# Two thin tiles of a mixture-of-experts stage: pinned on every engine, transposed through the score tiles, one weight tile in another buffer

## The chip, the core and the metric

The kernel runs on one core of a Trainium2 chip. The metric is the device time of one execution in microseconds (us). Before the change three executions took 421.13, 422.70 and 427.82 us; the median is 422.7 us. The execution that the profile was taken of is a further one: 420.79 us, of which the span from its first to its last instruction is 419.0 us.

## The reference

The inputs are q, k and v (4 batches, 8 heads, 768 positions, 64 wide), a decay per head, and the weights of a mixture of 8 experts. The first part is a decaying linear attention, worked in blocks. Its output is a matrix of 3072 tokens by 512. The second part sends each token to one expert:

```python
logits = x @ w_gate + modality_bias[modality_id]
e_idx = np.argmax(logits, axis=1)
...
for e in range(E):
    mask = e_idx == e
    h = np.maximum(x[mask] @ w1[e], 0.0)
    out[mask] = gate_w[mask, None] * (h @ w2[e])
```

w1 of one expert is 512 by 1024, w2 is 1024 by 512: 2 MB each in fp32.

## The kernel before, in words

**Stages.** The attention runs first, and the tokens are written to DRAM (`xs`) with their gate logits. On the way each token gets a slot in a table `inv`, sorted by expert. The second part goes over tiles of tokens of one expert. A wide tile has 256 tokens; a thin one has 64 (`XT`) or 32 (`FEW`). The order is: wide tile 0, wide tile 1, the two thin tiles, and then ten or more wide tiles. The change touches what stands between the layers of wide tile 1 and the first wide tile behind the thin ones: `run_early`.

**A wide tile** gathers its rows (POOL, indirect DMA into `xg`), transposes them on PE (L614) into the PSUM tiles `x` and `kv`, and splits them into a high and a low part (`xh` on ACT, `xl` on DVE). Its weights arrive in `raw1` and `raw2` and are split into `w1h`, `w1l` and `w2h`, `w2l` in four quarters each (ACT L553 the high part, DVE L554 the low part). Each product is then three matmuls (L627, L630, L631). The first layer writes the PSUM tiles `s`, the second layer `o`.

**A thin tile** uses plain fp32 and no split. `turn_few` transposes its rows (`xq` to `xf`). `thin_first` multiplies them by w1 (L662), several column strips side by side, and ACT applies the ReLU into `hn` (L666). `thin_turn` transposes `hn` on PE (L673), and DVE copies the result to `hnt` (L675). `thin_second` multiplies by w2 (L687), ACT scales it (L691) and POOL scatters it to the output (L695).

**Where weights of the thin tiles lie.** The 64-token tile takes its weights from `raw1` and `raw2`, where they arrive under a condition: if the tile has the same expert as the one before it, the transfer is skipped and the old contents serve. The 32-token tile's weights are always loaded. Before the change `fetch_both` puts its w1 in the buffer of `w1h` and its w2 in the buffer of `w1l`, which are free as soon as the first layer of wide tile 1 is over.

**Order.** Each engine executes its queue in order. `pinned` ties an instruction behind the last pinned one of its engine; what isn't pinned is placed by the scheduler of the framework. Weights are fetched by SP, whose queue is in order too: an instruction that waits there holds up all behind it. The first of the fetches in question waits until the gather of the next tile's rows has landed (`fetch_w1(..., gathered)`).

Of the kernel before, what the change touches and what calls it, by code (L numbers as in the profile page):

```python
# [6 lines left out]
F32 = mybir.dt.float32  # L7
F32R = mybir.dt.float32r
BF16 = mybir.dt.bfloat16
I32 = mybir.dt.int32  # L10
AF = mybir.ActivationFunctionType
# [4 lines left out]
P = 128  # L16
# [4 lines left out]
LOADS = 3  # L21
# [19 lines left out]
def linear_attention_moe(tc, qkv, lam, modality, wg, mbias, w1, w2, out):  # L41
    nc = tc.nc
    with ExitStack() as ctx:
# [10 lines left out]
        def behind(later, first, wait=True):  # L54

            info = (mybir.DependencyInfo(mybir.DependencyClass.Sync, mybir.DependencyReason.DATA) if wait else
                    mybir.DependencyInfo(mybir.DependencyClass.NoSync, mybir.DependencyReason.SCHED_ONLY))
            tc.add_manual_dep(later.ins, first.ins.name, info, reason="order")
# [493 lines left out]
        def split(src, hi, lo, pin=False):  # L552
            cp = nc.scalar.copy(out=hi, in_=src)  # L553
            df = nc.vector.tensor_tensor(out=lo, in0=src, in1=hi.bitcast(F32), op=ALU.subtract)  # L554
            if pin:
                pinned(cp)
                pinned(df)
            return cp, df
# [28 lines left out]
        def fetch_regs(lst, i, always):  # L587
            er = nc.sync.value_load(item(lst, 0, i), min_val=0, max_val=E - 1)
            if always:
                return er, {}  # L590
            cr = nc.sync.value_load(item(lst, 2, i), min_val=0, max_val=1)
            return er, {"cond": cr}
# [10 lines left out]
        def fetch_w1(er, kw, after=None, to=None):  # L603
            fetch_halves(raw1_all if to is None else to, w1, er, kw, after)

        def fetch_w2(er, kw, after=None, to=None):
            fetch_halves(raw2_all if to is None else to, w2, er, kw, after)
# [14 lines left out]
        def turn_rows(cols, before=None, part=range(2), pin=False):  # L622
            for i in part:
                split(*turn_part(i, cols, before, pin))
# [28 lines left out]
        def thin_first(x, w):  # L653

            m = x.shape[-1]
            ways = P // m
            hp = ps.tile([P, 8, P], F32, name="s", bufs=2)[:, : FC // ways]
            per = max(1, 4 // ways)
            for q in range(per):
                for kc in range(KC):  # L660
                    for fh in range(ways):
                        mm = nc.tensor.matmul(hp[fh * m : (fh + 1) * m, 2 * q : 2 * q + 2, :].rearrange("p a f -> p (a f)"),  # L662
                                              x[:, kc, :], w[per * fh + q][:, kc, :], start=(kc == 0), stop=(kc == KC - 1),
                                              tile_position=(0, fh * m))
            hn = work.tile([P, FC // ways, P], F32, name=f"hn{m}", bufs=1)
            nc.scalar.activation(out=hn, in_=hp, func=AF.Relu)  # L666
            return hn, mm

        def thin_turn(hn, mm):
            n = hn.shape[1]  # L670
            tp = ps.tile([P, n, P], F32, name=("x", "kv")[n // 4], bufs=1)
            for f in range(n):
                behind(nc.tensor.transpose(out=tp[:, f, :], in_=hn[:, f, :], identity=ident), mm, wait=False)  # L673
            hnt = work.tile([P, n, P], F32, name=f"hnt{n}", bufs=1)
            nc.vector.tensor_copy(out=hnt, in_=tp)  # L675
            return hnt

        def thin_second(idx, hnt, w2, m):

            ways = P // m  # L680
            w = DM // ways
            yp = ps.tile([P, w], F32, name="o", bufs=2)
            for f in range(FC):
                a, b = divmod(f, 2)
                fh, f4 = divmod(f, hnt.shape[1])
                for j in range(ways):
                    mm = nc.tensor.matmul(yp[j * m : (j + 1) * m], hnt[:, f4, fh * m : (fh + 1) * m],  # L687
                                          w2[a][:, b, j * w : (j + 1) * w], start=(f == 0), stop=(f == FC - 1),
                                          tile_position=(0, j * m))
            y = work.tile([P, w], F32, name=f"yn{m}", bufs=1)  # L690
            nc.scalar.activation(out=y, in_=yp, func=AF.Copy, scale=idx[:, 0, 1:2].bitcast(F32))  # L691
            to = work.tile([P, 1], I32, name="to", bufs=THIN)
            nc.vector.tensor_scalar(out=to, in0=idx[:, 0, 0:1], scalar1=float(ways), scalar2=strip[:, m // XT :][:, :1],
                                    op0=ALU.mult, op1=ALU.add)
            sc = nc.gpsimd.indirect_dma_start(  # L695
                out=out.rearrange("t (n w) -> (t n) w", n=ways),
                out_offset=bass.IndirectOffsetOnAxis(ap=to, axis=0),
                in_=y, in_offset=None, bounds_check=ways * N - 1, oob_is_err=False)
            apart("tokens", sc)
            return mm  # L700

        def second(idx, whole):
            for t in range(2):
# [32 lines left out]
        def turn_few(x, rows):  # L736
            m = x.shape[-1]
            tp = ps.tile([P, KC, m], F32, name=("x", "kv")[m // XT], bufs=1)
            for kc in range(KC):
                nc.tensor.transpose(out=tp[:, kc, :], in_=rows[:, kc * (P + E) : kc * (P + E) + P], identity=ident[:m, :m])  # L740
            return nc.vector.tensor_copy(out=x, in_=tp)

        def fetch_both(er, kw):

            first, second = parts(F32)
            second = second.rearrange("p i k f -> p i (k f)").rearrange("p i (f n) -> p i f n", f=2)
            fetch_w1(er, kw, to=first)
            fetch_w2(er, kw, to=second)
            return quarters(first), quarters(second)

        def quarters(t):
            return [t[:, i] for i in range(4)]
# [5 lines left out]
        def parts(dt):  # L758

            return [work.tile([P, 4, KC, TT], dt, name=nm, bufs=1) for nm in ("w1h", "w1l")]  # L760
# [187 lines left out]
        def regs(n):  # L948
            return fetch_regs(*tiles[n][1:], False)
# [8 lines left out]
        fixed_ones = EARLY + THIN + MIN_WIDE  # L958
        wides = EARLY + THIN
        idxs = {}  # L960
        before = None

        def rows_of(n):

# [5 lines left out]

        def run(n):
            idx = idxs.get(n) or get_idx(n)
            turned = wide(first_tail if n == 0 else tail, before, True)
            if n + 1 < fixed_ones:
                ahead = range(EARLY, wides + 1) if n == 0 else range(n + 2, min(n + 3, fixed_ones))
                if n == 0:
                    turn_rows(TT, turned, pin=True)
                    for i in range(4):
                        split(raw1[i], w1h[i], w1l[i], True)
                    late_list(*begun[2], exA, nA)  # L980
                    fetch_w2(*regs(n + 1))
                for m in ahead:
                    idxs[m] = get_idx(m)
                if n > 0:
                    fetch_w2(*regs(n + 1))
                    turn_rows(TT, turned, pin=True)
                for m in ahead:
                    gathered = rows_of(m)
                if n > 0:
                    for i in range(4):  # L990
                        split(raw1[i], w1h[i], w1l[i], True)
                if n + 2 < fixed_ones:
                    fetch_w1(*regs(n + 2), gathered)
            second(idx, turned)

        def run_early(n):

            nonlocal w1h, w1l, before
            idx = idxA[n]
            whole = wide(tail, pin=True)  # L1000
            fetch_w2(*regs(EARLY))
            both = fetch_both(*fetch_regs(*tiles[EARLY + 1][1:], True))
            turn_few(xf[0], xq[0])
            second(idx, whole)
            turn_few(xf[1], xq[1])
            hn, _ = thin_first(xf[0], raw1)
            fetch_w1(*regs(wides))
            other, mm = thin_first(xf[1], both[0])
            hnt = [thin_turn(hn, mm)]
            turn_rows(TT, part=(0,))  # L1010
            mm = thin_second(idxs[EARLY], hnt[0], raw2, XT)
            hnt.append(thin_turn(other, mm))
            turn_rows(TT, mm, part=(1,))
            gathered = rows_of(wides + 1)
            fetch_w2(*regs(wides))
            before = thin_second(idxs[EARLY + 1], hnt[1], both[1], FEW)
            w1h, w1l = (quarters(t) for t in parts(F32R))
            for i in range(4):
                split(raw1[i], w1h[i], w1l[i])
            fetch_w1(*regs(wides + 1), gathered)  # L1020

        for n in range(fixed_ones):
# [67 lines left out]
```

## Time and profile before

| | |
|---|---|
| median of three executions | 422.7 us (421.13 to 427.82) |
| profiled execution | 420.79 us, span 419.0 us |
| PE busy | 396.8 us (95% of the span) |
| DVE busy | 252.6 us (60%) |
| ACT busy | 181.3 us (43%) |
| POOL busy | 114.4 us (27%) |
| mean granted clock of TensorE | 0.985 |

PE is the matmul engine TensorE, PEld its weight loads, DVE VectorE, ACT ScalarE, POOL GpSimd, SP the engine that issues most transfers. A name such as L687 is a line of the kernel before. In rows of an engine's order, `o<-raw,hnt` means that the instruction writes `o` and reads `raw` and `hnt`; the profile's names leave out numbers, so `raw` is `raw1` or `raw2`. A bracket at a row's end tells how long the engine had been idle, and on whom it waited. A granted clock of 1.00 is TensorE's upper level, 2.4 GHz, and 0.50 its lower, 1.2 GHz.

### The profile page before, as it was taken

Reading aid. Unit: us, or ns where it says so; the run is one execution under the profiler, and the core shown is the slowest. Engines: PE = TensorE matmul, PEld = TensorE weight load, DVE = VectorE, ACT = ScalarE, POOL = GpSimd, SP = SyncE. Lnnn points to the kernel's source line nnn. Section 1 sums busy time; section 2 is a strip of 40 time slices with the busy share of each in tenths; the row PEclk is TensorE's granted clock in tenths of the full one; section 3 lists DMA queues with packets and bytes.
Section 4 is the critical chain, followed back from the end, with each engine's and each line's share of the span. In section 5 each row is a group of like instructions: output and inputs, shape, how many; then the busy total and the mean of one; then the engine's idle time right before and its main releaser. Section 6 shows DMA issues by size and latency. Waiting matters only on the chain.

```text
span 419.0 us, 9681 instructions
## 1 busy us (share of the span) xinstructions
PE 396.8 (95%) x3864; PEld 354.4 (85%) x3864; DVE 252.6 (60%) x435; ACT 181.3 (43%) x273; POOL 114.4 (27%) x117
## 2 busy tenths in 40 slices
PE   8799999999899999899999999999999999999970
PEld 4599999889798986698989899898989898998950
DVE  5678687879689731476473828374664838273600
ACT  1123323325446432455463827364555638273410
POOL 5010144263178530322040222213040402202010
PEclk9999999999899999999999999999999999999995
DMA  6999999995910129122026775302020111101010
GB/s 208 329 387 388 391 358 349 332 386 196 337 54 4 60 66 395 59 53 80 25 71 235 240 265 159 146 14 70 25 80 25 55 50 46 50 3 52 2 34 12
DMA packets 23348, 63.82 MB, mean 152 GB/s; under 512 B 6901, under 2 KB 8445, under 8 KB 21248
## 3 DMA queue, kind: packets, MB, share of 16 engines
q1 hardware_dynamic: 15056, 43.36, 28.8%
q0 software_dynamic: 4768, 13.08, 9.8%
q10 hardware_dynamic: 3472, 6.69, 4.1%
q8 instruction: 32, 0.52, 0.5%
q14 instruction: 20, 0.16, 0.1%
HBM read 91.40 MB, written 14.07 MB: 252 GB/s over the span
## 4 chain that ended last, share of the span: by engine, by line
issue 44%; POOL 9%; DMA 8%; SPq 2%; DVE 0%; POOLq 0%
POOL out_dram L711 6%; DMA idx<-inv 4%; DMA xg<-xs,idx 4%; POOL xg L579 3%; SPq L567 1%; SPq L597 1%; POOL out_dram L695 0%; SPq L564 0%; POOLq L579 0%; POOLq L711 0%; DVE ats L538 0%; DVE listB L540 0%; DVE atB L438 0%; SPq L569 0%; DVE listB L541 0%
## 5 line engine op out<-in xcount | busy, mean ns | idle before, releaser
L631 PE MATMUL s<-xh,w1l 128*128 128x256 f32 x384 | 107.8, 281 | 1.0 <-DVE w1l L554 1.0
L627 PE MATMUL s<-xh,w1h 128*128 128x256 f32 x384 | 108.1, 281 | 0.0
L630 PE MATMUL s<-xl,w1h 128*128 128x256 f32 x384 | 107.6, 280 | 0.0
L645 DVE SCALAR_TENSOR_TENSOR hl<-s,hh 128x512 fp32r<-128x512 f32 x48 | 33.2, 691 | 81.0 <-ACT hh L644 81.0
L627 PE MATMUL o<-w2h,hh 128*128 128x512 f32 x192 | 75.8, 395 | 0.0
L631 PE MATMUL o<-w2h,hl 128*128 128x512 f32 x192 | 74.8, 390 | 0.0
L630 PE MATMUL o<-w2l,hh 128*128 128x512 f32 x192 | 74.8, 389 | 0.0
L631 PEld LDWEIGHTS s<-xh,w1l 128*128 128x128 f32 x384 | 73.5, 191 | 1.2 <-DVE w1l L554 1.2
L627 PEld LDWEIGHTS s<-xh,w1h 128*128 128x128 f32 x384 | 72.2, 188 | 1.8 <-ACT hh L644 0.8
L630 PEld LDWEIGHTS s<-xl,w1h 128*128 128x128 f32 x384 | 72.1, 188 | 0.4
L554 DVE TENSOR_TENSOR w2l<-raw,w2h 128x1024 fp32r<-128x1024 f32 x48 | 58.8, 1224 | 10.6 <-ACT w2h L553 10.6
L644 ACT ACTIVATE hh<-s 128x512 fp32r<-128x512 f32 x48 | 28.8, 599 | 71.0 <-PE s L631 68.4
L711 POOL DMA_INDIRECT out_dram<-y,idx x20 | 28.1, 1403 | 98.2 <-ACT y L710 93.8
L554 DVE TENSOR_TENSOR w1l<-raw,w1h 128x1024 fp32r<-128x1024 f32 x46 | 53.4, 1219 | 0.9 <-PE o L687 0.8
L553 ACT CAST w2h<-raw 128x1024 fp32r<-128x1024 f32 x48 | 49.9, 1039 | 0.0
L579 POOL DMA_INDIRECT xg<-xs,idx x20 | 24.4, 1218 | 84.6 <-PE kv L614 79.7
L553 ACT CAST w1h<-raw 128x1024 fp32r<-128x1024 f32 x46 | 45.1, 1065 | 0.0
L631 PEld LDWEIGHTS o<-w2h,hl 128*128 128x128 f32 x192 | 36.0, 188 | 7.6
L630 PEld LDWEIGHTS o<-w2l,hh 128*128 128x128 f32 x192 | 36.1, 188 | 7.2
L627 PEld LDWEIGHTS o<-w2h,hh 128*128 128x128 f32 x192 | 36.1, 188 | 7.2
L389 POOL DMA_INDIRECT inv<-pay,sloti x24 | 32.8, 1365 | 23.0 <-PE x L296 5.6
L710 ACT ACTIVATE y<-o,idx 128x512 f32<-128x512 f32 x20 | 13.8, 690 | 52.4 <-PE o L631 42.5
(216 smaller groups left out, 472.1 us busy)
## 6 DMA issues: line engine op xcount, KB each, us to landing
raw<-in_w_dram SPq DMA_DIRECT2D x52, 1024.0 KB
load<-in_qkv_dram SPq DMA_DIRECT2D x11, 2048.0 KB
xs<-xn ACTq DMA_DIRECT2D x24, 272.0 KB
load<-in_qkv_dram SPq DMA_DIRECT2D x4, 512.0 KB
w1h<-in_w_dram SPq DMA_DIRECT2D x2, 1024.0 KB
w1l<-in_w_dram SPq DMA_DIRECT2D x2, 1024.0 KB
dk<-tab_d SPq DMA_DIRECT2D x2, 256.0 KB
inv<-pad SPq DMA_DIRECT2D x2, 196.0 KB
```

The costliest lines, as they stand in the source:

```text
L389: sc = nc.gpsimd.indirect_dma_start(out=inv, out_offset=bass.IndirectOffsetOnAxis(ap=at, axis=0), in_=pay[:, c, :], in_offset=None)
L553: cp = nc.scalar.copy(out=hi, in_=src)
L554: df = nc.vector.tensor_tensor(out=lo, in0=src, in1=hi.bitcast(F32), op=ALU.subtract)
L567: nc.sync.dma_start(out=idx[p : p + cols, 0, :], in_=inv[bass.ds(vr, cols), 0:2])
L579: last = nc.gpsimd.indirect_dma_start(out=(to or xg)[t][:m], out_offset=None, in_=xs[:rows, :], in_offset=bass.IndirectOffsetOnAxis(ap=idx ...
L627: mm = pinned(nc.tensor.matmul(out, ah, bh, start=first, stop=False))
L630: pinned(nc.tensor.matmul(out, ah, bl, start=False, stop=False))
L631: return pinned(nc.tensor.matmul(out, al, bh, start=False, stop=last))
L644: act = nc.scalar.activation(out=hh[i], in_=hp, func=AF.Relu)
L645: low = nc.vector.scalar_tensor_tensor(out=hl[i], in0=hp, scalar=0.0, in1=hh[i].bitcast(F32), op0=ALU.max, op1=ALU.subtract)
L710: nc.scalar.activation(out=y, in_=yp, func=AF.Copy, scale=idx[:, t, 1:2].bitcast(F32))
L711: sc = nc.gpsimd.indirect_dma_start(out=out, out_offset=bass.IndirectOffsetOnAxis(ap=idx[:, t, 0:1], axis=0), in_=y, in_offset=None, bound ...
```

## The change

All instructions of the thin tiles on PE, ACT and DVE are pinned in the order of the code. The transposes of `hn` go to PSUM tiles of the kind `s` instead of `x` and `kv`. The code of `run_early` is in another order: both first layers, then the transposes of both thin tiles with those of the next wide tile's rows, then its splits, then both second layers. The 32-token tile's w2 goes to a third buffer of the pool `load` (`w2f`), which no one else uses by then; its w1 stays in the buffer of `w1h`. Its w2 is now fetched ahead of the 64-token tile's w2, and its w1 behind it.

```diff
+            pinned(nc.scalar.activation(out=hn, in_=hp, func=AF.Relu))
...
-            tp = ps.tile([P, n, P], F32, name=("x", "kv")[n // 4], bufs=1)
+            tp = ps.tile([P, 8, P], F32, name="s", bufs=2)[:, :n]
...
             whole = wide(tail, pin=True)
+            few = fetch_regs(*tiles[EARLY + 1][1:], True)
+            w2f = work.tile([P, 4, 2, DM], F32, name="w2f", tag="load", bufs=LOADS)
+            fetch_w2(*few, to=w2f)
             fetch_w2(*regs(EARLY))
-            both = fetch_both(*fetch_regs(*tiles[EARLY + 1][1:], True))
+            w1f = work.tile([P, 4, KC, TT], F32, name="w1h", bufs=1)
+            fetch_w1(*few, to=w1f)
+            both = quarters(w1f), quarters(w2f)
             turn_few(xf[0], xq[0])
             second(idx, whole)
             turn_few(xf[1], xq[1])
-            hn, _ = thin_first(xf[0], raw1)
+            hns = [thin_first(xf[0], raw1)]
             fetch_w1(*regs(wides))
-            other, mm = thin_first(xf[1], both[0])
-            hnt = [thin_turn(hn, mm)]
-            turn_rows(TT, part=(0,))
-            mm = thin_second(idxs[EARLY], hnt[0], raw2, XT)
-            hnt.append(thin_turn(other, mm))
-            turn_rows(TT, mm, part=(1,))
+            hns.append(thin_first(xf[1], both[0]))
+            hnt = [thin_turn(hns[0])]
+            parts0 = turn_part(0, TT, pin=True)
+            hnt.append(thin_turn(hns[1]))
+            parts1 = turn_part(1, TT, pin=True)
+            split(*parts0)
+            split(*parts1)
+            w1h, w1l = (quarters(t) for t in parts(F32R))
+            split(raw1[0], w1h[0], w1l[0], True)
+            split(raw1[1], w1h[1], w1l[1], True)
+            thin_second(idxs[EARLY], hnt[0], raw2, XT)
             gathered = rows_of(wides + 1)
             fetch_w2(*regs(wides))
-            before = thin_second(idxs[EARLY + 1], hnt[1], both[1], FEW)
-            w1h, w1l = (quarters(t) for t in parts(F32R))
-            for i in range(4):
-                split(raw1[i], w1h[i], w1l[i])
+            split(raw1[2], w1h[2], w1l[2], True)
+            thin_second(idxs[EARLY + 1], hnt[1], both[1], FEW)
+            split(raw1[3], w1h[3], w1l[3], True)
             fetch_w1(*regs(wides + 1), gathered)
```

**PE between the layers of wide tile 1 and the next wide tile.** `hn64` and `hnt4` belong to the 64-token tile, `hn32` and `hnt2` to the 32-token tile; `w1h` in an L662 row holds the small tile's w1. Before:

```order
L662 MATMUL s_2459<-raw1_122,xf0_138 64x256 x16
L614 MATMUL x_2524<-ident_91,xg0_126 128x128
...
L662 MATMUL s_2498<-w1h_2381,xf1_139 32x256 x16
L673 MATMUL kv_2517<-ident_91,hn64_2476 128x128 x4
L687 MATMUL o_2531<-raw2_123,hnt4_2522 64x256 x16
L673 MATMUL x_2555<-ident_91,hn32_2515 128x128 x2
L614 MATMUL kv_2560<-ident_91,xg0_126 128x128
...
L687 MATMUL o_2604<-w1l_2382,hnt2_2558 32x128 x32
```

and now:

```order
L662 MATMUL s_2459<-raw1_122,xf0_138 64x256 x16
L1027 TENSOR_LOAD nums_151
L662 MATMUL s_2498<-w1h_2384,xf1_139 32x256 x16
L673 MATMUL s_2517<-ident_91,hn64_2476 128x128 x4
L614 MATMUL x_2524<-ident_91,xg0_126 128x128
...
L673 MATMUL s_2529<-ident_91,hn32_2515 128x128 x2
L614 MATMUL kv_2534<-ident_91,xg0_126 128x128
...
L687 MATMUL o_2549<-raw2_123,hnt4_2522 64x256 x16
L687 MATMUL o_2612<-w2f_2361,hnt2_2532 32x128 x32
```

The small tile's first layer comes directly behind the other's, all transposes stand together, and both second layers stand last.

**SP, the fetches for the thin tiles**, of which each row left out is a second half of the same transfer or a register instruction. Before:

```order
L597 DMA raw1_122<-in_w1_dram 128x2048
...
L597 DMA raw2_123<-in_w2_dram 128x2048
...
L597 DMA w1h_2381<-in_w1_dram 128x2048
...
L597 DMA w1l_2382<-in_w2_dram 128x2048
...
L569 DMA idx5_2567<-inv_114 128x2x2
```

and now:

```order
L597 DMA raw1_122<-in_w1_dram 128x2048
...
L597 DMA w2f_2361<-in_w2_dram 128x2048
...
L597 DMA raw2_123<-in_w2_dram 128x2048
...
L597 DMA w1h_2384<-in_w1_dram 128x2048
...
L569 DMA idx5_2573<-inv_114 128x2x2
```

The small tile's w2 has moved ahead by one place, and its w1 is now the last of the four.

## Rows read from the trace of the kernel before

**Rows 1.** PE idle by cause from 170 us on: engine, line, releaser: us, times, longest.

```profile
PE s L631 <- DVE w1l L554: 1.0, 1, 1.0
```

**Rows 2.** One stretch: length, busy us by engine, granted clock, DMA share, GB/s.

```profile
180.00:190.00 10.00, 10.00 (x80) 9.62 (x80) 7.41 (x9) 6.50 (x10) 2.10 (x3) 1.00 0.16 37
```

**Rows 3.** PE in order of time: start us, us, engine, line, operation, tiles, shapes, count.

```profile
160.30 0.43 PE L740 MATMUL x<-ident,xq 32*128 32x32 f32 x4
160.66 3.67 PE L662 MATMUL s<-raw,xf 128*64 128x256 f32 x32
164.27 0.66 PE L614 MATMUL x<-ident,xg 128*128 128x128 f32 x4
164.85 1.93 PE L662 MATMUL s<-w1h,xf 128*32 128x256 f32 x32
166.72 0.66 PE L673 MATMUL kv<-ident,hn 128*128 128x128 f32 x4
168.16 3.67 PE L687 MATMUL o<-raw,hnt 128*64 128x256 f32 x32 [0.78 <-DVE hnt L675]
171.76 0.44 PE L673 MATMUL x<-ident,hn 128*128 128x128 f32 x2
172.04 0.60 PE L614 MATMUL kv<-ident,xg 128*128 128x128 f32 x4
172.72 1.96 PE L687 MATMUL o<-w1l,hnt 128*32 128x128 f32 x64
174.60 0.39 PE L627 MATMUL s<-xh,w1h 128*128 128x256 f32 x1
...
176.08 0.39 PE L631 MATMUL s<-xh,w1l 128*128 128x256 f32 x1 [0.97 <-DVE w1l L554]
```

**Rows 4.** The same view of SP's transfer issues.

```profile
153.93 1.35 SPq L597 DMA_DIRECT2D raw<-in_w_dram  x4
155.51 0.93 SPq L597 DMA_DIRECT2D w1h<-in_w_dram  x2
156.71 1.23 SPq L597 DMA_DIRECT2D w1l<-in_w_dram  x2
```

**Rows 5.** The queue SP fills, 155 us to 164.3, then to 169.95: packets, MB, share.

```profile
q1 hardware_dynamic: 350, 2.61, 76.0%
...
q1 hardware_dynamic: 848, 4.20, 74.0%
```

**Rows 6.** Short stretches, columns as in rows 2: the transfers' rate stands last.

```profile
153.40:153.90 0.50, 0.50 (x4) 0.41 (x3) 0.00 (x0) 0.00 (x0) 0.00 (x0) 1.00 0.00 0
163.00:164.00 1.00, 1.00 (x14) 0.59 (x10) 0.00 (x0) 0.00 (x0) 0.00 (x0) 1.00 1.08 451
169.00:169.50 0.50, 0.50 (x8) 0.29 (x5) 0.00 (x0) 0.00 (x0) 0.00 (x0) 1.00 0.31 67
169.50:170.00 0.50, 0.50 (x8) 0.35 (x6) 0.00 (x0) 0.00 (x0) 0.00 (x0) 1.00 0.00 0
```

**Rows 7.** PE idle by cause in the whole span, two rows.

```profile
PE kv L252 <- DVE kd L212: 2.6, 1, 2.6
PE x L614 <- DMA xg<-xs,idxA: 1.9, 1, 1.9
```

**Rows 8.** The clock around the first and the second, columns as in rows 2.

```profile
10.00:20.00 10.00, 7.39 (x90) 5.07 (x90) 5.70 (x7) 0.92 (x4) 1.15 (x4) 1.00 0.91 313
...
109.00:114.00 5.00, 4.38 (x30) 3.70 (x31) 2.37 (x5) 3.06 (x4) 2.00 (x2) 0.66 1.00 365
```

**Rows 9.** DVE in order of time, columns as in rows 3.

```profile
150.47 1.23 DVE L554 TENSOR_TENSOR w2l<-raw,w2h 128x1024 fp32r<-128x1024 f32 x1 [0.15 <-ACT w2h L553]
...
167.41 0.69 DVE L675 COPY hnt<-kv 128x512 f32<-128x512 f32 x1 [1.14 <-PE kv L673]
...
174.80 1.23 DVE L554 TENSOR_TENSOR w1l<-raw,w1h 128x1024 fp32r<-128x1024 f32 x1 [0.81 <-PE o L687]
```

**Rows 10.** ACT in order of time, columns as in rows 3.

```profile
173.16 1.05 ACT L553 CAST w1h<-raw 128x1024 fp32r<-128x1024 f32 x1
```

More of the change, by code (lines that the diff above doesn't have):

```diff
@@ L661, in thin_first, with thin_turn @@
                     for fh in range(ways):
-                        mm = nc.tensor.matmul(hp[fh * m : (fh + 1) * m, 2 * q : 2 * q + 2, :].rearrange("p a f -> p (a f)"),
-                                              x[:, kc, :], w[per * fh + q][:, kc, :], start=(kc == 0), stop=(kc == KC - 1),
-                                              tile_position=(0, fh * m))
+                        pinned(nc.tensor.matmul(hp[fh * m : (fh + 1) * m, 2 * q : 2 * q + 2, :].rearrange("p a f -> p (a f)"),
+                                                x[:, kc, :], w[per * fh + q][:, kc, :], start=(kc == 0), stop=(kc == KC - 1),
+                                                tile_position=(0, fh * m)))
             hn = work.tile([P, FC // ways, P], F32, name=f"hn{m}", bufs=1)
-            nc.scalar.activation(out=hn, in_=hp, func=AF.Relu)
-            return hn, mm
-        def thin_turn(hn, mm):
+            pinned(nc.scalar.activation(out=hn, in_=hp, func=AF.Relu))
+            return hn
+        def thin_turn(hn):
             n = hn.shape[1]
-            tp = ps.tile([P, n, P], F32, name=("x", "kv")[n // 4], bufs=1)
+            tp = ps.tile([P, 8, P], F32, name="s", bufs=2)[:, :n]
             for f in range(n):
-                behind(nc.tensor.transpose(out=tp[:, f, :], in_=hn[:, f, :], identity=ident), mm, wait=False)
+                pinned(nc.tensor.transpose(out=tp[:, f, :], in_=hn[:, f, :], identity=ident))
             hnt = work.tile([P, n, P], F32, name=f"hnt{n}", bufs=1)
-            nc.vector.tensor_copy(out=hnt, in_=tp)
+            pinned(nc.vector.tensor_copy(out=hnt, in_=tp))
             return hnt
@@ L686, in thin_second @@
                 for j in range(ways):
-                    mm = nc.tensor.matmul(yp[j * m : (j + 1) * m], hnt[:, f4, fh * m : (fh + 1) * m],
-                                          w2[a][:, b, j * w : (j + 1) * w], start=(f == 0), stop=(f == FC - 1),
-                                          tile_position=(0, j * m))
+                    pinned(nc.tensor.matmul(yp[j * m : (j + 1) * m], hnt[:, f4, fh * m : (fh + 1) * m],
+                                            w2[a][:, b, j * w : (j + 1) * w], start=(f == 0), stop=(f == FC - 1),
+                                            tile_position=(0, j * m)))
             y = work.tile([P, w], F32, name=f"yn{m}", bufs=1)
-            nc.scalar.activation(out=y, in_=yp, func=AF.Copy, scale=idx[:, 0, 1:2].bitcast(F32))
+            pinned(nc.scalar.activation(out=y, in_=yp, func=AF.Copy, scale=idx[:, 0, 1:2].bitcast(F32)))
             to = work.tile([P, 1], I32, name="to", bufs=THIN)
@@ L699, in thin_second @@
             apart("tokens", sc)
-            return mm
         def second(idx, whole):
@@ L739, in turn_few @@
             for kc in range(KC):
[L740 to L749, printed above, removed]
+                pinned(nc.tensor.transpose(out=tp[:, kc, :], in_=rows[:, kc * (P + E) : kc * (P + E) + P],
+                                           identity=ident[:m, :m]))
+            return pinned(nc.vector.tensor_copy(out=x, in_=tp))
         def quarters(t):
@@ L960, in linear_attention_moe @@
         idxs = {}
-        before = None
         def rows_of(n):
@@ L972, in run @@
             idx = idxs.get(n) or get_idx(n)
-            turned = wide(first_tail if n == 0 else tail, before, True)
+            turned = wide(first_tail if n == 0 else tail, pin=True)
             if n + 1 < fixed_ones:
@@ L996, in run_early @@
         def run_early(n):
-            nonlocal w1h, w1l, before
+            nonlocal w1h, w1l
             idx = idxA[n]
             whole = wide(tail, pin=True)
+            few = fetch_regs(*tiles[EARLY + 1][1:], True)
+            w2f = work.tile([P, 4, 2, DM], F32, name="w2f", tag="load", bufs=LOADS)
+            fetch_w2(*few, to=w2f)
             fetch_w2(*regs(EARLY))
-            both = fetch_both(*fetch_regs(*tiles[EARLY + 1][1:], True))
+            w1f = work.tile([P, 4, KC, TT], F32, name="w1h", bufs=1)
+            fetch_w1(*few, to=w1f)
+            both = quarters(w1f), quarters(w2f)
             turn_few(xf[0], xq[0])
```

## The prediction

> **What bounds the kernel now.** I began with the waits of PE. From 170 us to the end PE waits for another engine once, 1.0 us long [rows 1], and in a stretch behind that it is busy 10.00 of 10 us at a granted clock of 1.00 [rows 2]. So the ten wide tiles that follow the thin ones run on PE alone, and whatever the thin tiles gain or lose on PE reaches the end one for one. Then I read PE's own timeline of the stage [rows 3]. It begins at 160.30 us, when the second layer of wide tile 1 is over, and the next wide tile starts at 174.60, with one more stop before 176.08. The brackets give the two stops: 0.78 us, where the 64-token tile's second layer waits for DVE to copy `hnt`, and 0.97 us, where the wide tile waits for `w1l`. The rest is work. **1.75 us** is all that an order of instructions can win here, 0.4% of the span. Last come the transfers [rows 4 to 6], since the change reorders them too.
>
> **What it wins.** The first stop is a chain without cover: transposes of `hn`, a DVE copy of 0.69 us [rows 9], then the matmuls that read it. Now ten transposes stand between: starts in rows 3 give 0.58 us for the first four of the next tile (164.27 to 164.85), 0.28 for the two of `hn32` (171.76 to 172.04) and 0.68 for the other four (172.04 to 172.72), together 1.54 us. They cover the copy, so the 0.78 us go. The second stop comes of a buffer. The small tile's w2 lay in that of `w1l`, so DVE could begin to split only at 174.80, behind the last matmul that read it [rows 3, 9]. With w2 elsewhere a quarter's split (ACT 1.05 us, DVE 1.23 [rows 9, 10]) can begin when the small tile's first layer has released `w1h`. All that PE does from there to the wide tile (transposes of 0.5 us and those 1.54, second layers of 3.60 and 1.88 by the starts in rows 3) takes 7.5 us and hides two quarters; ACT scales the outputs in between, and the last two quarters are due only later, inside the wide tile. So the 0.97 us go as well.
>
> **What it costs.** The small tile's first layer needs its w1 in the buffer of `w1h`, and SP now asks for w2 first. SP stands still until 153.93, then issues four conditional halves in 1.35 us, 0.42 apart, then w1 from 155.51, then w2 [rows 4]. The conditional four move nothing: the queue carries 4.20 MB from 155 us on, which is two loads of 2 MB [rows 5]. By 164.3 it has carried 2.61 MB [rows 5], and w1 (2.1 MB) is used from 164.85 without a wait [rows 3]: the loads come in the order in which they are asked for. The bytes of the last end by 169.5 [rows 6]. One who waits hears of it about 0.4 us later: a gather's bytes had ended by 153.4, and SP, which waited for it, went on at 153.93 [rows 4, 6]. So the fourth half is to be had at 169.9.
>
> After the change that fourth half is part of w1. The train starts earlier by the two conditional halves that now stand behind w2, 0.84 us, and ends at about **169.06**. PE, with the transposes moved away, wants w1 at 164.27, the end of the other tile's first layer [rows 3]. Its matmuls take the four quarters of w1 in turn, so the third already needs the second half, and only 2 of 32 (0.12 us) can run ahead. PE idles 4.79 us, less 0.12: **+4.67**. With the two stops won: 4.67 - 1.75 = **+2.9 us**. What PE does behind the wait is what it did before.
>
> Bounds: if the train does not start earlier, 169.9 gives +3.8; if it ends 0.8 sooner than I take it, as with the lag counted nought and a little more rate, +2.1.
>
> One rule of the Trainium skill speaks against this term. DMA: Bandwidth & Descriptors (Anatomy of one DMA — SWDGE (gpsimd) path) fits a transfer as 2.0 us plus its bytes at 436 GB/s, measured on the software path. By that, as an estimate, w1 would be there some 11.6 us after the first issue, near 166.3, and the sum would be +0.2. The trace disagrees: from 155.51 to 169.9 the same bytes took 14.4 us.
>
> **The clock.** The trace has two waits of PE of like size. Behind one of 1.9 us the granted clock falls: its mean over 109 to 114 us is 0.66, that is (1 - 0.66) x 5 = 1.7 us lost. In the ten us that hold the one of 2.6 us it stays at 1.00 [rows 7, 8]. The new wait is longer than either, and two matmuls in its middle hardly break it. I take it to cost what the first did, **+1.7 us**; the ends are 0, as at the second, and 2.6, if PE runs low for half as long again.
>
> **The rest.** That `hn` is transposed into `s`: two buffers, and both were read by ACT before; PE finds the first free during the cover above. DVE copies `xf` of the 64-token tile behind its last `w2l` split, which starts at 150.47 and takes 1.23 us [rows 9], and it is wanted at 160.66 [rows 3]: 8.5 us of cover, and nothing if that were gone but the copy itself. On POOL half of a gather now stands ahead of an output's scatter and half between two; its rows are wanted only at the end of the wide tile's first layer, and the weights that SP fetches behind it later still. SP's register loads for later tiles shift by some rows, where no PE wait shows in the trace [rows 1]. All of these: 0.
>
> **Sum.** +2.9 and +1.7 is **+4.6 us** on the profiled execution of 420.8: 425.4. The median of the runs shown is 422.7, 1.9 above that execution, which would give 427.3. I say **426.3**, between the two, as one of the three runs agrees with the profiled one and one is far above it.
>
> **Rivals.**
>
> *Late w1, no loss of clock.* For it, the wait of 2.6 us that cost none; against it, that this one is nearly twice as long. 420.8 + 2.9 = 423.7, or 424.7 on the same middle footing. Chance 0.30.
>
> *w1 is in time.* The order of instructions wins its 1.75 us: 419.0 on the profiled footing, 420.0 on the middle one. It needs w1 complete by 164.3. At the best rate in rows 6, 451 GB/s, 4.2 MB take 9.3 us; with a start near 155.7 and the lag, w1 comes at 165.4, and 420.0 to 421.0 comes out. By the rows the loads would have to do over the whole train what they do in their best us. Chance 0.11. The fit of the Trainium skill's page DMA: Bandwidth & Descriptors, told above, lies between this and the last one, near 421.
>
> *Slower by more than 2%.* The thin stage stays at the lower clock. Behind the wait PE has 1.8 us of the small tile's first layer and 7.5 us more to do [rows 3]. All of it at 1.2 GHz costs 9.3 us more: 2.9 + 9.3 = 12.2, and 433 us. It decides from a loss of 5.5 us on, which is 11 us at the lower level. Against it: the loss in rows 8 amounts to 3.4 us at that level, after which it was back. Chance 0.06.
>
> *The forecast*, late w1 with the clock lost once, has the remaining 0.53.
>
> **How the numbers follow.** 2% of the median, about what a measurement of this kernel can tell from no change, is 8.4 us. The forecast and both first rivals lie within it. Faster by over 2% needs more than there is to win: 0.01. Slower by over 2%: the third rival, 0.06. Same: 0.93. The range takes in the forecast with its clock term at 2.6 and its landing at the upper end on the median's footing (422.7 + 3.8 + 2.6 = 429.1), and the second case with its lower bound on the profiled footing (420.8 + 2.1 = 422.9); down to 421.5 it takes half of the third. It leaves out the rest of that and the slow one.
>
> **What would show it.** Right: PE's timeline has one idle stretch of 4 to 5.5 us between the two L662 groups, released by a DMA on `w1h`; the brackets in front of the 64-token L687 and of the wide tile's first L631 are gone; behind the wait a stretch with a granted clock of 0.50; the wide tile starts some 3 to 6 us later than at 174.60. Wrong: `w1h` lands before 165 us, or PE runs other work during the wait, or a new stop stands before the wide tile because its splits come too late.

## The result and the profile after

The changed kernel takes **427.44 us** (median of 20 executions, 423.43 to 431.16), the kernel before 423.16 (20 executions beside them, 420.04 to 427.82). The ratio is **1.0083 [1.0062, 1.0105]**: 3.5 us slower [2.6, 4.4]. It leaves out executions that lie far above the fastest, five of the change's twenty, and so is below the quotient of the two medians, 1.0101. The forecast was 426.3 us, 1.0085 of the median of before that it had, 422.7.

The profiled execution of the change took 424.42 us, of which the span is 422.7. PE's timeline of the stage of [rows 3], after the change; "..." stands for rows left out, and the last row is the first of the second wide tile behind the thin ones:

```profile
163.59 0.43 PE L739 MATMUL x<-ident,xq 32*128 32x32 f32 x4
163.95 3.67 PE L662 MATMUL s<-raw,xf 128*64 128x256 f32 x32
167.87 0.63 PE L662 MATMUL s<-w1h,xf 128*32 128x256 f32 x4 [0.24 <-DMA w1h<-in_w_dram]
170.73 1.92 PE L662 MATMUL s<-w1h,xf 128*32 128x256 f32 x28 [2.23 <-DMA w1h<-in_w_dram]
172.58 0.66 PE L673 MATMUL s<-ident,hn 128*128 128x128 f32 x4
...
174.26 3.67 PE L687 MATMUL o<-raw,hnt 128*64 128x256 f32 x32
177.87 1.96 PE L687 MATMUL o<-w2f,hnt 128*32 128x128 f32 x64
179.75 0.38 PE L627 MATMUL s<-xh,w1h 128*128 128x256 f32 x1
...
180.09 0.32 PE L631 MATMUL s<-xh,w1l 128*128 128x256 f32 x1
...
202.76 0.28 PE L627 MATMUL s<-xh,w1h 128*128 128x256 f32 x1
```

The brackets of 0.78 and 0.97 us are gone, and two new ones stand at the small tile's first layer, both released by the transfer into `w1h`. They are 0.24 and 2.23 us long, where 4 to 5.5 were expected. From 172.58 to the end PE waits for nothing that has a bracket. SP's issues, to be held against [rows 4]:

```profile
155.78 0.53 SPq L597 DMA_DIRECT2D raw<-in_w_dram  x2
156.54 0.93 SPq L597 DMA_DIRECT2D w2f<-in_w_dram  x2
157.81 0.52 SPq L597 DMA_DIRECT2D raw<-in_w_dram  x2
158.61 1.25 SPq L597 DMA_DIRECT2D w1h<-in_w_dram  x2
```

The small tile's w1 is now the last of the train, as I call the four fetches. DVE and ACT, to be held against [rows 9, 10]; columns as there:

```profile
173.28 1.08 DVE L675 COPY hnt<-s 128x512 f32<-128x512 f32 x2 [8.92 <-PE s L673]
...
175.94 2.36 DVE L554 TENSOR_TENSOR w1l<-raw,w1h 128x1024 fp32r<-128x1024 f32 x2 [0.26 <-ACT w1h L553]
```
```profile
174.85 2.00 ACT L553 CAST w1h<-raw 128x1024 fp32r<-128x1024 f32 x2
```

The copy of `hnt` starts 1.0 us ahead of the second layer that reads it, and two quarters of the next weights are split by 178.3, before the wide tile wants them at 180.09.

The granted clock in stretches (columns as in [rows 2]) shows the other surprise. Behind the wait it stays at 1.00. It had fallen earlier, ahead of the stage, behind a wait for `cntB`, a tile that DVE makes; the profile of before doesn't have that wait, and lost its 1.7 us of clock at another place [rows 8]:

```profile
128.90:132.40 3.50, 3.50 (x10) 2.73 (x9) 3.50 (x9) 3.50 (x5) 2.63 (x3) 0.51 0.05 8
...
170.00:175.00 5.00, 4.27 (x50) 2.95 (x52) 1.72 (x4) 1.60 (x4) 0.50 (x1) 1.00 0.03 7
```
```profile
PE kv L614 <- DVE cntB L408: 2.1, 1, 2.1
```

So this one execution cannot tell the change alone: PE reaches the thin part at 163.59 instead of 160.30, for reasons ahead of it. In both kernels DVE, ACT and POOL do the same work in the same order up to 149 us, so nothing that was moved on them is that reason. The fair measure is the **stage**, from the transposes of the 32-token tile's rows (160.30 in [rows 3]) to the first matmul of the second wide tile behind the thin ones. Its first part, up to the next wide tile, I call the thin part. Behind the stage the time to the end of the last matmul is 207.2 us in every profile of this study. The kernel before has in these rows the fourth matmul of the first wide tile's first layer, the end of that layer, and the end of the stage:

```profile
176.30 0.28 PE L627 MATMUL s<-xh,w1h 128*128 128x256 f32 x1
...
187.65 0.48 PE L627 MATMUL o<-w2h,hh 128*128 128x512 f32 x1
...
198.65 0.28 PE L627 MATMUL s<-xh,w1h 128*128 128x256 f32 x1
```

Before: 198.65 - 160.30 = 38.35 us, of which 14.30 up to the next wide tile (174.60) and 24.05 in it. After: 202.76 - 163.59 = 39.17, of which 16.16 and 23.01. The stage lost 0.82 us in this execution, while the median lost 3.5.

### The profile page after: what moved, and what is told of

Its sections match the earlier page's. It is cut to its first block, busy times and chain, and to the rows that moved or that the text cites. A ratio compares the mean times of both kernels' runs of the same rounds, so it can differ in the third digit from the quotient of the medians.

```text
span 422.7 us, 9682 instructions
## 1 busy us (share of the span) xinstructions
PE 399.1 (94%) x3864; PEld 355.2 (84%) x3864; DVE 251.8 (60%) x435; ACT 181.2 (43%) x273; POOL 111.4 (26%) x117
## 4 chain that ended last, share of the span: by engine, by line
issue 35%; PE 31%; DMA 13%; POOL 7%; DVE 6%; SPq 2%; ACT 1%; another core or an unknown queue 1%; POOLq 0%; DVEq 0%
PE s L232 5%; PE x L296 5%; POOL out_dram L710 5%; PE o L285 5%; DMA idx<-inv 4%; PE o L278 3%; DMA w1h<-in_w_dram 3%; DMA xg<-xs,idx 2%; POOL xg L579 2%; PE s L627 2%; PE s L630 2%; PE kv L252 2%; PE s L631 2%; DMA xg<-xs,idxA 2%; DVE w1l L554 2%
## 5 line engine op out<-in xcount | busy, mean ns | idle before, releaser
L389 POOL DMA_INDIRECT inv<-pay,sloti x24 | 30.7, 1280 | 27.3 <-PE x L296 7.3
```

Source lines behind the costliest of these rows:

```text
L389: sc = nc.gpsimd.indirect_dma_start(out=inv, out_offset=bass.IndirectOffsetOnAxis(ap=at, axis=0), in_=pay[:, c, :], in_offset=None)
```

## The experiments

Theory A is the prediction's own: the small tile's w1 lands late because of the order of the fetches, and that alone makes the change slower; the rest of it gains. Nine further runs were made: seven edited kernels, and the change and the kernel before once more. Each has its stage from its own profile and its time against the kernel before (the difference in us goes by the ratio and the median of before that was measured beside it, 420 to 424 us).

| kernel | ratio [95%] | us by the ratio | thin part + wide tile = stage | stage against 38.35 |
|---|---|---|---|---|
| the change, first profile | 1.0083 [1.0062, 1.0105] | +3.5 | 16.16 + 23.01 = 39.17 | +0.82 |
| the change again | 1.0111 [1.0060, 1.0162] | +4.7 | 19.37 + 22.80 = 42.17 | +3.82 |
| before again | 0.9987 [0.9954, 1.0020] | -0.5 | 14.31 + 24.05 = 38.36 | +0.01 |
| change, w1 first | 0.9908 [0.9874, 0.9942] | -3.9 | 13.42 + 22.80 = 36.22 | -2.13 |
| before, w2 first | 1.0164 [1.0119, 1.0209] | +6.9 | 20.77 + 24.40 = 45.17 | +6.82 |
| change, w1 ahead of all | 0.9948 [0.9915, 0.9982] | -2.2 | 12.99 + 22.80 = 35.79 | -2.56 |
| before, third buffer | 0.9987 [0.9957, 1.0017] | -0.5 | 14.30 + 23.90 = 38.20 | -0.15 |
| order, old buffer | 0.9981 [0.9952, 1.0010] | -0.8 | 13.32 + 24.05 = 37.37 | -0.98 |
| change, wait half filled | 1.0091 [1.0052, 1.0130] | +3.8 | 20.06 + 23.20 = 43.26 | +4.91 |
| change, wait filled | 1.0064 [1.0036, 1.0092] | +2.7 | 17.85 + 23.00 = 40.85 | +2.50 |

**The change again, and the kernel before again.** No edit.

> The changed kernel once more, for a second profile of it. Theory A: the wait for w1 is there again, 2 to 5 us, larger where PE reaches the stage earlier, since the loads hang on the gather and not on PE; ratio 1.006 to 1.011. If the wait in a second profile is under 1 us while the ratio holds, theory A is wrong. A second question is whether PE's wait of 2.1 us for cntB, far ahead of the stage, is there again: if it belongs to the change, it is; if it is chance, it need not be.

> The kernel before against itself, for a second profile: ratio 0.998 to 1.002. Theory A: no wait for w1 in the thin stage, and the stops of 0.78 and 0.97 us are there. The start of the stage (160.3 us in the first profile) and the place where the clock falls may differ by 1 to 3 us; if they do, the 3.3 us by which the changed kernel's profile reaches the stage later is chance.

A second profile of the change looks like the forecast. PE's timeline:

```profile
162.79 3.67 PE L662 MATMUL s<-raw,xf 128*64 128x256 f32 x32
168.14 0.63 PE L662 MATMUL s<-w1h,xf 128*32 128x256 f32 x4 [1.68 <-DMA w1h<-in_w_dram]
171.16 3.09 PE L662 MATMUL s<-w1h,xf 128*32 128x256 f32 x28 [2.39 <-DMA w1h<-in_w_dram]
174.18 1.12 PE L673 MATMUL s<-ident,hn 128*128 128x128 f32 x4
```

Here the brackets sum to 4.07 us, and behind them the same 28 matmuls take 3.09 us instead of 1.92. The clock by stretches and SP's first issue:

```profile
171.80:175.20 3.40, 3.40 (x25) 1.84 (x18) 0.00 (x0) 0.38 (x1) 0.00 (x0) 0.50 0.00 0
```
```profile
156.09 0.53 SPq L597 DMA_DIRECT2D raw<-in_w_dram  x2
156.85 0.93 SPq L597 DMA_DIRECT2D w2f<-in_w_dram  x2
```

3.4 us at 0.50 of the clock, 1.2 GHz, cost 1.7. The profile has no wait for `cntB` and lost no clock ahead of the stage. The ratio, 1.0111, lies at the upper end of what was expected. The kernel before, a second time, repeated both of its stops and its stage to 0.01 us.

**The order of the fetches undone**, alone, in the changed kernel:

```diff
             few = fetch_regs(*tiles[EARLY + 1][1:], True)
-            w2f = work.tile([P, 4, 2, DM], F32, name="w2f", tag="load", bufs=LOADS)
-            fetch_w2(*few, to=w2f)
             fetch_w2(*regs(EARLY))
             w1f = work.tile([P, 4, KC, TT], F32, name="w1h", bufs=1)
             fetch_w1(*few, to=w1f)
+            w2f = work.tile([P, 4, 2, DM], F32, name="w2f", tag="load", bufs=LOADS)
+            fetch_w2(*few, to=w2f)
```

> The change with one thing undone: the small tile's w1 is fetched ahead of its w2 again, in its old place behind the conditional fetches; pins, transposes and the third load buffer stay. Theory A (the loss is PE's wait for w1, which stands behind w2 in SP's queue): the wait of 2.5 us in front of the small tile's first layer shrinks to 0 to 0.5 us, the two stops of 0.78 and 0.97 us stay away, and the ratio to the kernel before is 0.994 to 0.999. Theory B (the wait hardly counts: in the two profiles the stage itself differs by under 1 us, and the loss lies elsewhere, in the pins, the buffers or ahead of the stage): the ratio stays at 1.004 or more.

Faster than before: 0.9908, better than the 0.994 to 0.999 expected, and no wait of PE in the stage. One group still shows that w1 is barely in time: its 32 matmuls take 2.35 us instead of 1.93.

```profile
163.05 2.35 PE L662 MATMUL s<-w1h,xf 128*32 128x256 f32 x32
```

**The order of the fetches alone**, in the kernel before:

```diff
-            fetch_w1(er, kw, to=first)
             fetch_w2(er, kw, to=second)
+            fetch_w1(er, kw, to=first)
```

> The kernel before with one thing of the change: w2 of the small tile is fetched ahead of its w1, into the same two buffers as before. Theory A: PE wants w1 at 164.85 and has it at about 169 to 170, a wait of 2 to 5 us in front of the small tile's first layer, with the stops of 0.78 and 0.97 us still there; ratio to the kernel before 1.005 to 1.012. Theory B: the ratio is 1.000 to 1.003.

Two lines exchanged make the kernel 1.0164 times as long. PE's timeline has the change's new waits and the old stops together:

```profile
165.47 0.63 PE L662 MATMUL s<-w1h,xf 128*32 128x256 f32 x4 [1.98 <-DMA w1h<-in_w_dram]
168.28 3.25 PE L662 MATMUL s<-w1h,xf 128*32 128x256 f32 x28 [2.18 <-DMA w1h<-in_w_dram]
...
173.20 3.67 PE L687 MATMUL o<-raw,hnt 128*64 128x256 f32 x32 [0.78 <-DVE hnt L675]
```

The waits of 1.98 and 2.18 us are as expected; the ratio is above the 1.005 to 1.012 expected, which had no loss of clock in it, and the clock stood at 0.50 for 3.4 us here. With the kernel above this settles theory A from both sides.

**w1 ahead of everything**, the best version by its stage. The small tile's w1 is the first of the train and its w2 the last. The edit does one thing more: the 64-token tile's w1 is now fetched without the wait for the next gather, so the whole train starts earlier, 7.9 us ahead of the stage (150.29 to 158.18) and not 6.4 (153.93 to 160.30):

```diff
-                if n + 2 < fixed_ones:
+                if 0 < n < fixed_ones - 2:
...
-            w2f = work.tile([P, 4, 2, DM], F32, name="w2f", tag="load", bufs=LOADS)
-            fetch_w2(*few, to=w2f)
-            fetch_w2(*regs(EARLY))
             w1f = work.tile([P, 4, KC, TT], F32, name="w1h", bufs=1)
             fetch_w1(*few, to=w1f)
+            fetch_w1(*regs(EARLY))
+            fetch_w2(*regs(EARLY))
+            w2f = work.tile([P, 4, 2, DM], F32, name="w2f", tag="load", bufs=LOADS)
+            fetch_w2(*few, to=w2f)
```

> A better version: as the change, but the small tile's w1 is the first of the fetches, ahead of the conditional ones and of SP's wait for the gather, and its w2 the last. It asks whether anything of w1's arrival is left in the kernel with w1 fetched ahead of w2 (0.991 of the kernel before). Theory A (there w1 came just in time, about when PE wanted it): no wait for w1, the stage as long as there within 0.5 us, ratio 0.989 to 0.996. Rival (w1 was still late there in some executions): 1 to 2 us better than that, 0.985 to 0.989.

PE's timeline of the stage up to the wide tile's second layer; no row has a bracket, nor has one of those left out:

```profile
158.18 0.43 PE L739 MATMUL x<-ident,xq 32*128 32x32 f32 x4
158.54 3.67 PE L662 MATMUL s<-raw,xf 128*64 128x256 f32 x32
162.14 1.93 PE L662 MATMUL s<-w1h,xf 128*32 128x256 f32 x32
164.01 0.66 PE L673 MATMUL s<-ident,hn 128*128 128x128 f32 x4
...
165.68 3.68 PE L687 MATMUL o<-raw,hnt 128*64 128x256 f32 x32
169.29 1.95 PE L687 MATMUL o<-w2f,hnt 128*32 128x128 f32 x64
171.17 0.38 PE L627 MATMUL s<-xh,w1h 128*128 128x256 f32 x1
...
171.63 0.28 PE L627 MATMUL s<-xh,w1h 128*128 128x256 f32 x1
...
182.97 0.48 PE L627 MATMUL o<-w2h,hh 128*128 128x512 f32 x1
```

0.9948, and a stage 2.56 us shorter, within 0.5 us of that with w1 first, as theory A expected. This kernel shows what the order of the engines and the buffer are worth when w1 is no question. The kernel with w1 first, above, was measured 1.8 us better than its stage says (-3.9 [-5.3, -2.4] against -2.13); where the rest of that comes from I did not find, and I don't rank the two by their ratios.

**The third buffer alone**, in the kernel before:

```diff
-            first, second = parts(F32)
-            second = second.rearrange("p i k f -> p i (k f)").rearrange("p i (f n) -> p i f n", f=2)
+            first = work.tile([P, 4, KC, TT], F32, name="w1h", bufs=1)
+            second = work.tile([P, 4, 2, DM], F32, name="w2f", tag="load", bufs=LOADS)
```

> The kernel before with one part of the change: the small tile's w2 lies in the third load buffer; order of fetches and of the engines as before. Theory A: the stop of 0.97 us in front of the wide tile goes, the one of 0.78 us stays, no wait for w1; ratio 0.997 to 0.999. Rival (the splits of w1 come late for another reason, as they stand unpinned behind the small tile's second layer): the stop stays and the ratio is 1.000.

Same time. The stop of 0.97 us shrinks to 0.42 but stays. PE, then DVE:

```profile
173.63 0.39 PE L627 MATMUL s<-xh,w1h 128*128 128x256 f32 x1
...
174.55 0.38 PE L631 MATMUL s<-xh,w1l 128*128 128x256 f32 x1 [0.42 <-DVE w1l L554]
174.77 0.28 PE L627 MATMUL s<-xh,w1h 128*128 128x256 f32 x1
...
186.52 0.48 PE L627 MATMUL o<-w2h,hh 128*128 128x512 f32 x1
```
```profile
173.27 1.23 DVE L554 TENSOR_TENSOR w1l<-raw,w1h 128x1024 fp32r<-128x1024 f32 x1 [0.26 <-ACT w1h L553]
```

The buffer was free, and still the split came at 173.27. That is 13.94 us behind the stage's start at 159.33, only 0.56 sooner than in [rows 9] (174.80 - 160.30): in the unpinned order it stands behind the rows' split and the output's scaling. So the rival was right about the stop, and theory A was not. Of the 0.55 us won at the stop the wide tile keeps only 0.15. The other 0.4 is given back behind it, where no bracket shows it: from the fourth matmul to the end of the first layer it takes 186.52 - 174.77 = 11.75 us, and 187.65 - 176.30 = 11.35 in the kernel before.

**The order alone**: w1 first as above, but w2 in the buffer of `w1l` again:

```diff
-            w2f = work.tile([P, 4, 2, DM], F32, name="w2f", tag="load", bufs=LOADS)
-            fetch_w2(*few, to=w2f)
             fetch_w2(*regs(EARLY))
-            w1f = work.tile([P, 4, KC, TT], F32, name="w1h", bufs=1)
+            w1f, w2f = parts(F32)
+            w2f = w2f.rearrange("p i k f -> p i (k f)").rearrange("p i (f n) -> p i f n", f=2)
             fetch_w1(*few, to=w1f)
+            fetch_w2(*few, to=w2f)
```

> The change without its third buffer: pins, the order of the engines and the transposes in score tiles as changed, the small tile's w1 fetched ahead of its w2, and w2 in the buffer of w1l as before. Theory A: the stop of 0.78 us is gone, a stop of about 1 us in front of the wide tile is back, no wait for w1; ratio 0.997 to 1.000. Rival (order and pins are worth more than their stop, since the kernel with all but the fetch order gained 3.9 us where the two stops are 1.75): ratio 0.991 to 0.995.

As theory A expected, the ratio is between 0.997 and 1.000, the stop of 0.78 is gone and that for `w1l` is back in PE's waits:

```profile
PE s L631 <- DVE w1l L554: 1.0, 1, 1.0
```

**The wait filled**, with matmuls (128x512, bf16) whose result no one uses, between the two first layers of the change: 12 in the one kernel, 22 in the other. Their work is no part of the computation.

```diff
+            keep_busy(12)
             hns.append(thin_first(xf[1], both[0]))
```

> The change with twelve idle matmuls of 128x512 (about 2.6 us of PE at full clock, nothing reads them) between the first layers of the two thin tiles, where PE waits for w1. They add no path of their own as long as the wait is over 2.6 us. Theory C (PE's idling costs the clock, 1.7 us): the granted clock stays at 1.00 behind the wait, and from the start of wide tile 1 to the end of the wide tile behind the thin ones it takes 62.5 to 64 us, where the second profile of the change had 65.1; ratio to the kernel before 1.004 to 1.008. Rival (the clock falls for another reason, or its fall costs little): 0.50 for 3.4 us behind the wait as before, 64.5 us or more, ratio 1.009 or more.

> As the kernel with twelve idle matmuls, now with twenty-two of them (about 5 us, the whole of the wait, which there was 5.4 us from PE's arrival to the landing of w1's second half). There 2.1 us of the wait were left behind the filling, and the clock fell behind them. Theory C (idling in the wait costs the clock, 1.7 us): the wait left is under 1 us, the granted clock stays at 1.00 through the stage, and from the start of wide tile 1 to the end of the wide tile behind the thin ones it takes 64 to 65 us, against 66.2 with twelve; ratio 1.004 to 1.008. Rival (the clock falls whatever PE does there): 0.50 behind it again and 66 us or more, ratio 1.009 to 1.012.

PE's timeline with 12 (first fence; the trace lacks one of their records) and with 22:

```profile
162.11 2.76 PE L790 MATMUL o<-busy 128*128 128x512 bf16 x11
164.83 0.63 PE L662 MATMUL s<-w1h,xf 128*32 128x256 f32 x4
167.56 3.27 PE L662 MATMUL s<-w1h,xf 128*32 128x256 f32 x28 [2.10 <-DMA w1h<-in_w_dram]
```
```profile
168.72 4.92 PE L790 MATMUL o<-busy 128*128 128x512 bf16 x22
173.57 1.93 PE L662 MATMUL s<-w1h,xf 128*32 128x256 f32 x32
```

Twelve did not cover it: 2.10 us of wait were left, and the clock fell behind them for 3.4 us all the same, the outcome expected of the rival; but with a wait left it doesn't decide between the two. With 22, as theory C expected, PE idles nowhere in the stage, and the clock stays up (12.00 of 12 us busy, granted 1.00):

```profile
168.00:180.00 12.00, 12.00 (x104) 6.73 (x102) 3.62 (x6) 4.04 (x6) 1.05 (x1) 1.00 0.32 114
```

The second stage is 2.4 us shorter than the first, although it holds 2.2 us more of useless work. That fits a clock loss that hangs on idle time, but the execution with 22 also came late to the stage, as the first profile of the change did, so the two differ in more than the filling.

## Why the prediction was right, point by point

**The landing: right.** The mechanism was the one forecast: w1 comes last in the train, and PE stops for it. The forecast had it at 169.06, that is 15.13 us behind SP's first issue at 153.93. Measured: 170.73 - 155.78 = 14.95 and 171.16 - 156.09 = 15.07. The Trainium skill (DMA: Bandwidth & Descriptors, Anatomy of one DMA — SWDGE (gpsimd) path) would have the 4.2 MB, as an estimate, done 11.6 us after the first transfer that is not skipped. The traces disagree: 170.73 - 156.54 = 14.2, 171.16 - 156.85 = 14.3, and 14.3 in the kernel before with w2 first (issue at 154.02, use at 168.28). The rival with w1 in time started its train near 155.7 and left out the 0.84 us of the sum; no profile comes near its 165.4 either way.

**PE's arrival: right in one profile, not in the other.** In the trace of before PE wanted w1 at 164.27, 10.34 us behind SP's first issue. In the second profile of the change it is 168.14 - 1.68 - 156.09 = 10.37, and the fill kernel with 12 has 10.04. In the first profile it is 167.87 - 0.24 - 155.78 = 11.85, and with 22 it is 168.72 - 156.84 (SP's first issue there) = 11.88. In the other five profiles whose train waits for the gather it is 9.92 to 10.40. Just the two late ones have a wait of 2.1 and 1.9 us for `cntB` and a loss of 1.7 us of clock at 129 us, ahead of the stage; SP's train hangs on a gather, PE's arrival on all that PE does before. That the one loss makes the other is likely by its size, and not shown. Both are profiles of the changed kernel, one with fillers, and the two others of that kind have neither; whether the change has a part in it is open. So the term of **+4.67** was 171.16 - 166.46 - 0.24 = **4.46** in the second profile, and 170.73 - 167.63 - 0.24 = **2.86** in the first. The 0.24 was 0.12 in the prediction, which counted two of 32: two of the 16 instructions ran ahead, and each has two rows in the trace. The term is not a constant of the kernel but a race, decided by some 1.5 us that differ between two profiles of the same kernel.

**What it wins: too small.** I gave 1.75 us, "all that an order of instructions can win here". Both stops did go, but the stage without waits is 2.56 shorter. Two wins were missed. The four groups of transposes cost 0.58 + 0.66 + 0.28 + 0.68 = 2.20 us by the starts in [rows 3] (without the stop of 0.78); standing together they take 165.68 - 164.01 = 1.67: **0.53**. And the stop of 0.97 us cost more than its bracket. The wide tile's first layer takes 182.97 - 171.17 = 11.80 us instead of 187.65 - 174.60 = 13.05, that is 1.25 less, **0.28** beyond the bracket. All of it lies at the stop: the fourth matmul starts 171.63 - 171.17 = 0.46 behind the first without it and 176.30 - 174.60 = 1.70 with it, and from there on both take 11.34 and 11.35. 0.78 + 0.97 + 0.53 + 0.28 = 2.56. The attribution was incomplete too: I put the 0.97 down to the buffer. The buffer alone left a stop of 0.42, the order alone all of it; only both together take it away.

**The clock: right in one profile.** +1.7 was 1.7 in the second profile (3.4 us at 0.50) and nothing in the first. That the rival without a loss got 0.30 was fair.

**The sum.** Second profile: 4.46 + 1.7 - 2.56 = +3.6, measured +3.82, forecast +4.6. First profile: 2.86 - 2.56 = +0.3, measured +0.82. In the first, 0.21 of the rest lies in the wide tile (23.01 against 22.80). The medians, +3.5 [2.6, 4.4] and +4.7 [2.5, 6.8], side with the second; how often executions go as the first did, two profiles of the change can't say. The forecast of +4.6 is a little above the interval of the first ratio, by the wins that were missed. The median came out 1.1 above the forecast all the same, since the median of before beside it, 423.16, stands 1.5 above the 421.7 to which I had added the 4.6. That the forecast's 1.0085 stands so close to the measured 1.0083 is luck: 426.3 is 421.7 + 4.6 but was divided by 422.7, and over its own start it is 1.0109. The prediction also took 2% for what a measurement of this kernel can tell from no change; the intervals in the table are 0.2 to 0.5% to each side, so 3.5 us can be told from no change.

## What to carry to other kernels

Moving a consumer forward on a busy engine and its load backward in an in-order queue is one change with two halves: put both on one clock, from the queue's release, before counting what the order wins. When a gain needs a free buffer and an early producer, try each alone; here neither took the stop of 0.97 us away, and both together did. And don't take a bracket for the whole price of a stop: here each stop for `w1l` cost some 0.25 us more. Where a wait is the difference of two chains that don't hang on each other, profile the same kernel twice before believing its size.

## What the runs showed of the hardware that was not expected

- **The clock does not fall by the length of a wait alone.** It fell to 0.50 for 3.4 us behind waits of 2.10, 2.18 and 1.68 + 2.39 us for w1, and it stayed at 1.00 behind 0.24 + 2.23 us of the same wait in the first profile. Upstream it stayed at 1.00 behind the longest wait of all, 3.29 us for `kd`, in the second profile (first row and its stretch below), and fell behind one of 1.78 for the same tile in the kernel with 22 fillers (second pair). What decides is open.

```profile
16.48 0.69 PE L252 MATMUL kv<-load,kd 128*64 128x64 f32 x16 [3.29 <-DVE kd L212]
...
16.40:20.40 4.00, 3.92 (x68) 3.39 (x70) 2.27 (x4) 0.59 (x1) 0.62 (x1) 1.00 0.94 333
```
```profile
16.00 0.69 PE L252 MATMUL kv<-load,kd 128*64 128x64 f32 x16 [1.78 <-DVE kd L212]
...
16.80:20.20 3.40, 3.40 (x32) 3.00 (x31) 1.99 (x3) 0.00 (x0) 0.62 (x1) 0.51 1.08 383
```

- **A stop of PE costs more than its idle time.** In the five profiles with the stop for `w1l` the fourth matmul of the wide tile starts 0.25 to 0.27 us later than the bracket accounts for; the rows above give 1.70 - 0.46 - 0.97 = 0.27 for the kernel before.

- **The same first layer runs at more than one pace, without a stop.** From its fourth matmul to the second layer it takes 11.34 to 11.36 us in six profiles (the kernel before twice, the change's second, both kernels with w1 earlier, and the old buffer) and 11.75 in three (before with w2 first, before with the third buffer, the wait half filled), all at a granted clock of 1.00. In the two others it takes 11.52. Why is open.
